# Row sends moved out of the ends of two outer stages, into the last inverse and the first 28 expert tiles

## The chip, the cores and the metric

One core of a Trainium2 chip runs the kernel. The metric is the device time of one execution in microseconds. The kernel before took 2111.44 us, the median of 3 runs (2107.42 to 2115.52).

## The reference

Two parts run one after the other. The first is a long convolution over 4 batches of 11456 tokens with 128 channels, done with transforms: `u = x * v`, its transform times the transform of a filter `h_filt` made by a small network from `pos_emb`, transformed back to `y`, cut to the sequence, and `x * y` handed on. The second is a mixture of 8 experts over the 45824 tokens: `logits = x @ w_gate + modality_bias[modality_id]`, the expert of a token is the `argmax`, `gate_w` its softmax weight, and `out = gate_w * (relu(x @ w1[e]) @ w2[e])` for the tokens of expert `e`.

## The kernel before

**The convolution.** A transform is split in two. An outer stage runs 16 steps q over the channels; a middle stage runs 23 groups g (`NG`) of frequencies. Outer stage b (0 to 4) does two things in one step: `product` and `transform` bring batch b in, and `inverse` (`turn`, `transform` of `inverse_stages`) takes batch b-1 out. Outer stage 0 has no inverse, outer stage 4 (the last inverse) has no product. Between outer stage b and the next stands middle stage b: `spectrum` (PE L646), `products` (DVE L663 and L670; POOL L665, L666, L676, L677), `inverse` (PE L701). With the inverse runs the routing of its tokens, one block `o` of 16 columns in two steps: `shift` on POOL (L808, L810) prepares the biases in `lg`, `biased` on DVE (L817) adds the logits to them, `choice` finds the expert, `send` computes where each token's row goes, and `store` writes rows to DRAM (`xr`).

**The rows.** The finished rows of a batch have to be put in the order of their expert, in `xs`. A batch has 90 pieces of 128 rows, numbered here batch.piece (0.0 to 3.89): 360 sends. `send_rows` (L283) is an indirect DMA that POOL issues; it takes a piece from `waiting`, reads it from one of three `back` tiles, each of 5 pieces, and writes it to `xs`. The load of a `back` tile (`rows_back`, L263) is issued on POOL too, behind the second piece of the tile before it. `paced` sends n pieces that also wait for a given DVE instruction. A batch comes into `waiting` (`fetch`) once its rows are stored and at most 5 pieces are left of the batch before. Sends stand at four kinds of places:

- in outer stages 2 and 3, `product` sends 2 or 3 a step and `inverse` 1 on each of two DVE instructions (L743, L746);
- in middle stages 2 and 3, `products` sends 7 in all, from group 13 on;
- in the last inverse, `inverse` sends 2 or 3 a step;
- in the expert part, a tile sends 4 until tile 12 and 3 afterwards, until all are gone.

**The experts.** Tiles of 512 rows of one expert run through 8 chunks c of the hidden layer. PE, ACT and DVE work on a tile; SP reads its rows (`x<-xs`, L1121 or L1125), writes its result `oT` to `ob` and reads it back as `y` (2 buffers). POOL multiplies `y` by the gate (L1290) and issues 4 indirect DMAs of results, `out<-ot` (L1292). The first 37 tiles (`NW0`) need batches 0 and 1 only, so the first `x<-xs` waits for sends 0.0 to 1.89; tiles to 59 need three batches. From tile 50 on, `rest` waits for all 360 sends, writes rows of padding behind each expert's rows (SP, L1052 and L1060) and makes the table for the tiles from 60 on. Those writes stand on SP's queue ahead of the rows of tile 53.

**What sets the order.** The order on PE, ACT, DVE and SP is that in which the program is written. POOL's is not: a scheduler places its instructions, and a send that the program writes in a middle stage can stand ahead of that stage's first products.

Of the kernel before, what the change touches and what calls it, by code (L numbers as in the profile page):

```python
# [67 lines left out]
NDYN = 8  # L68
NA, NXO = 12, 3
NPE = 9  # L70


def apart(a, axis):
# [116 lines left out]
def hyena_moe_kernel(ctx: ExitStack, tc: tile.TileContext, a: dict, out: bass.AP,  # L190
                     nb: int = B, nt: int = NF + NH):
    nc = tc.nc
    pe, act, dve, pool, sp = nc.tensor, nc.scalar, nc.vector, nc.gpsimd, nc.sync
# [14 lines left out]
    def bank(name):  # L208
        return banks[-1].tile([D, 512], F32, tag="ps", name=name)
# [7 lines left out]
    def sm(name):  # L217
        lo, hi = SMALL[name]
        return small[:, lo:hi]
# [22 lines left out]
    def ins_of(x):  # L242
        return getattr(x, "ins", x)
# [21 lines left out]
    def fetch(b):  # L265

        sp.dma_start(to_t[b % 2], xi[b].rearrange("(p c) -> p c", p=D))
        rows_back(b, 0)
        waiting.extend((b, c) for c in range(NR // D))
# [109 lines left out]
    with ExitStack() as cv:  # L379
# [5 lines left out]
        def pair(name):  # L385
            return pairs.tile([D, 2, 512], F32, tag="pp", name=name)
# [4 lines left out]
        def new_a(key):  # L391

            taken[key] = tiles.pop(0)
            return taken[key]

        def free(*keys):

            tiles.extend(taken.pop(key) for key in keys)
# [62 lines left out]
        def xo_of(b, o):  # L461

            return xo_t[(NO * b + o) % NXO]

        def paced(x, n=1):

            send_rows(n, wait=ins_of(x))

        def four(src, w=2):

            return src.rearrange("p (w n d) -> p w n d", w=w, n=4)

        def forward_stages(b):
            kept = {}

            def load(q):
                for name in ("u", "v"):
                    if b == 0 and name == "v":
                        of = xo_t[q // 2 % NXO].rearrange("p w s h r -> p (w s h r)")
                        t = of[:, 1024 * (q % 2):1024 * (q % 2) + 1024]  # L480
                    else:
                        t = new_a((name, q))
                    kept[q, name] = t
                    sp.dma_start(t[0:D:2], a[name][b, q, 0:D // 2])
                    sp.dma_start(t[1:D:4], a[name][b, q, D // 2:])

            def product(q):

                u = kept[q, "u"]
                s = dve.scalar_tensor_tensor(u, u, sm("held")[:, 0:1], kept.pop((q, "v")),  # L490
                                             op0=ALU.mult, op1=ALU.mult)
                paced(s, 2 + (q % 2 == 0))
                if b:
                    free(("v", q))

            def transform(q):

                u = kept.pop((q, "u")).rearrange("p (b d n) -> p b d n", b=2, n=N2)
                for h in range(2):
                    p = pair("s1")  # L500
                    v = p[:, :, 0:4 * N1].rearrange("p b (d k) -> p b d k", d=4)
                    for j in range(4):
                        for blk in range(2):
                            for c in range(2):
                                pe.matmul(v[64 * c:64 * c + 64, blk, j], u[:, blk, 4 * h + j],  # L505
                                          fwd[:, c], start=True, stop=True)
                    d0 = 8 * q + 4 * h
                    act.copy(A.rearrange("p k b d -> p b k d")[:, :, :, d0:d0 + 4],
                             v.rearrange("p b d k -> p b k d"))
                free(("u", q))  # L510

            return load, product, transform
# [204 lines left out]
        def inverse_stages(b):  # L717

            kept = {}
            w_of = lambda q, blk: w_t[blk + 2 * (q % 2 if b == nb - 1 else 0)]  # L720

            def load(q):
                t = kept[q] = new_a(("x", q))
                sp.dma_start(t, a["x"][b, q])

            def turn(q, blk):
                for c in range(2):
                    p = bank("wt")
                    for j in range(4):
                        pe.transpose(p[0:N1, D * j:D * j + D], A[:, :, blk, 8 * q + 2 * j + c], ident)  # L730
                    act.copy(w_of(q, blk)[:, c], p[0:N1])

            def transform(q):


                py = pair("py")
                for c in range(2):
                    for blk in range(2):
                        pe.matmul(py[64 * blk:64 * blk + 64, c], inv[:, c], w_of(q, blk)[:, c],
                                  start=True, stop=True)  # L740
                y = new_a(("y", q))
                act.copy(y[:, 512:1024], py[:, 1])
                paced(dve.tensor_add(y[:, 0:512], py[:, 0], y[:, 512:1024]),  # L743
                      1 + (b == nb - 1 and q % 2))
                dve.tensor_sub(y[:, 512:1024], py[:, 0], y[:, 512:1024])
                paced(dve.tensor_mul(xo_of(b, q // 2)[:, :, q % 2, :, 0:D], four(y),  # L746
                                     four(kept.pop(q))))
                free(("x", q), ("y", q))

            return load, turn, transform  # L750
# [329 lines left out]
    kept = {}  # L1080
# [10 lines left out]
    def experts(lo, hi):  # L1091
# [5 lines left out]
        def rows_in(i):  # L1097
# [10 lines left out]

            by_pe = k["by_pe"] = i < NPE or i == last or n < T
            x = mt.tile([D, 4, RW], F32, tag="x", name="x", bufs=4)  # L1110
# [193 lines left out]
        for at in range(len(work) + 6):  # L1304
            i, c = work[at] if at < len(work) else (last + 1, at - len(work))
            if c == 0:
                rows_in(i + 2)
            hidden(at)
            if at < 2:
                weights(lo, 2 + at)  # L1310
            if lo == 0 and 0 <= at - FL < len(finale):
                finale[at - FL](late)
            if lo == 0 and at >= FL + len(finale) + 2 and len(waiting) <= RC and not fetched:
                fetched.append(fetch(nb - 1))
            if lo == 0 and c % (2 if i < 12 else 3) == 0:
                send_rows(1)
            if lo == 0 and 1 <= i and c % 3 == 0:
                whole_weights(1)
            if 8 <= i < NW0:
                next(second, 0)  # L1320
            if NW1 - 10 <= i < NW1:
                next(others, 0)
            if c < 4:
                weights(i + 1, c)
            result(at - 3)
            whole = i <= last and tiles[i][2] == T
            if c == (3 if whole else 1):
                rows_turn(i + 1)
            if c == (4 if whole else 2):
                rows_split(i + 1)  # L1330
            if c == 2 and i - 2 in by_act:
                rows_out(i - 2)
            if c == (5 if whole else 3) and i - 1 not in by_act:
                rows_out(i - 1)
# [52 lines left out]
```

## Time and profile before

| | |
|---|---|
| median of 3 runs | 2111.44 us (2107.42 to 2115.52) |
| profiled execution | 2110.57 us, span 2108.7 us |
| mean granted TensorE clock | 0.986 |
| PE busy | 2022.3 us, 96% |
| DVE busy | 1675.1 us, 79% |
| POOL busy | 1369.1 us, 65% |
| ACT busy | 1192.9 us, 57% |
| 360 sends `xs<-back` on POOL (L283) | 389.4 us busy, 1082 ns each |
| 362 issues `out<-ot` on POOL (L1292) | 392.1 us busy, 1083 ns each |

The busy share of POOL is a mean over stages: in the expert part it has hardly a gap while rows are sent, at other times it waits. In rows of the trace the bracket at the end is the time that the engine sat idle before the instruction, and what released it. "issue" there is time in which it waited for nothing that the profile shows. Outer stage 2 ends at about 610 us, outer stage 3 at about 863 us; the last inverse runs from about 985 to 1075 us.

### The profile page before, as it was taken

How to read it: one execution, taken by the hardware profiler on the slowest of the kernel's cores; microseconds unless marked ns; L12 is line 12 of the kernel's file. 1: busy time of each engine (PE TensorE's matmuls, PEld its weight loads, DVE VectorE, ACT ScalarE, POOL GpSimd, SP SyncE). 2: the span in 40 equal slices, each digit the busy share in tenths (PEclk: the TensorE clock that was granted, in tenths of full speed). 3: DMA queues.
4: the chain of work that ended last, by engine and by line, in shares of the span. 5: the costliest groups of instructions: out<-in, count | busy, mean ns of one | idle time of the engine just before them, and what ended most of it. 6: DMA issues, size and time to landing. Idle time of an engine off the chain costs nothing. (4 is left out here: it accounts for less than half of the span.)

```text
span 2108.7 us, 49645 instructions
## 1 busy us (share of the span) xinstructions
PE 2022.3 (96%) x17794; PEld 1653.7 (78%) x17794; DVE 1675.1 (79%) x2663; ACT 1192.9 (57%) x2174; POOL 1369.1 (65%) x1496
## 2 busy tenths in 40 slices
PE   8999999999978999699999999999999999999997
PEld 8887877777757877488668888888888888888897
DVE  2538867996767967497887899988999999899885
ACT  3642476226631266223766666666666666666775
POOL 2219600796778876787667887888888665555554
PEclk9999999999989999899999999999999999999998
DMA  9846766678975788666689466666655554554310
GB/s 290 304 167 237 244 205 185 229 250 271 286 234 190 255 267 278 195 228 215 182 261 305 106 132 131 133 133 134 136 132 125 122 113 96 100 99 99 81 41 30
DMA packets 502932, 380.74 MB, mean 181 GB/s; under 512 B 374745, under 2 KB 408365, under 8 KB 502681
## 3 DMA queue, kind: packets, MB, share of 16 engines
q1 hardware_dynamic: 470265, 294.16, 51.0%
q0 software_dynamic: 32256, 83.33, 11.8%
q8 instruction: 142, 2.33, 0.4%
q14 instruction: 109, 0.89, 0.1%
q10 hardware_dynamic: 160, 0.03, 0.0%
HBM read 273.80 MB, written 103.96 MB: 179 GB/s over the span
## 5 line engine op out<-in xcount | busy, mean ns | idle before, releaser
L1240 DVE SCALAR_TENSOR_TENSOR hl<-ph,hh 128x512 fp32r<-128x512 f32 x724 | 484.7, 680 | 93.9 <-ACT hh L1239 85.0
L1239 ACT ACTIVATE hh<-ph 128x512 fp32r<-128x512 f32 x724 | 424.5, 598 | 200.9 <-PE ph L1236 193.1
L283 POOL DMA_INDIRECT xs<-back,to x360 | 389.4, 1082 | 175.8 <-issue 87.2
L1292 POOL DMA_INDIRECT out<-ot,idx x362 | 392.1, 1083 | 128.6 <-issue 82.0
L1234 PE MATMUL ph<-xh,wh 128*128 128x512 f32 (+1 forms) x792 | 298.5, 377 | 1.1 <-ACT xh L1220 1.1
L1236 PE MATMUL ph<-xl,wh 128*128 128x512 f32 (+1 forms) x792 | 296.1, 374 | 2.4 <-DVE xl L1221 2.4
L1235 PE MATMUL ph<-xh,wl 128*128 128x512 f32 (+1 forms) x792 | 294.4, 372 | 1.0 <-DVE wl L1189 1.0
L1257 PE MATMUL po<-hh,wh 128*128 128x512 f32 (+1 forms) x792 | 294.4, 372 | 0.0
L1259 PE MATMUL po<-hl,wh 128*128 128x512 f32 (+1 forms) x792 | 293.9, 371 | 0.0
L1258 PE MATMUL po<-hh,wl 128*128 128x512 f32 (+1 forms) x792 | 293.7, 371 | 0.0
L701 PE MATMUL pw<-rings,a 64*128 64x128 f32 x3952 | 242.1, 278 | 38.0 <-POOL a L676 33.9
L701 PEld LDWEIGHTS pw<-rings,a 64*128 64x128 f32 x3952 | 230.6, 191 | 57.3 <-POOL a L676 36.4
L707 ACT COPY A<-pw 128x512 f32<-128x512 f32 x180 | 95.7, 584 | 317.7 <-PE pw L701 317.7
L670 DVE TENSOR_TENSOR a<-pz,rings 128x1024 f32<-128x1024 f32 (+1 forms) x184 | 211.5, 1191 | 1.0 <-POOL a L677 1.0
L646 PE MATMUL pz<-A,rings 128*64 128x256 f32 x1440 | 170.0, 384 | 13.4 <-issue 8.9
L1236 PEld LDWEIGHTS ph<-xl,wh 128*128 128x128 f32 x792 | 149.4, 189 | 31.0 <-DVE xl L1221 3.5
L505 PE MATMUL s<-fwd,a 128*64 128x90 f32 x4096 | 170.1, 242 | 1.2 <-issue 1.1
L1235 PEld LDWEIGHTS ph<-xh,wl 128*128 128x128 f32 x792 | 149.6, 189 | 26.3 <-DVE wl L1189 1.3
L1234 PEld LDWEIGHTS ph<-xh,wh 128*128 128x128 f32 x792 | 149.4, 189 | 26.3 <-ACT xh L1220 1.3
L1257 PEld LDWEIGHTS po<-hh,wh 128*128 128x128 f32 x792 | 149.1, 188 | 26.0 <-issue 0.7
L1259 PEld LDWEIGHTS po<-hl,wh 128*128 128x128 f32 x792 | 149.1, 188 | 25.8
L1258 PEld LDWEIGHTS po<-hh,wl 128*128 128x128 f32 x792 | 149.1, 188 | 25.3
(192 smaller groups left out, 3537.7 us busy)
## 6 DMA issues: line engine op xcount, KB each, us to landing
rings<-hs SPq DMA_DIRECT2D x88, 512.0 KB
a<-in_x SPq DMA_DIRECT2D x64, 512.0 KB
xr<-xo SPq DMA_DIRECT2D x64, 365.6 KB
back<-xr POOLq DMA_DIRECT2D x72, 325.0 KB
rings<-in_c_b SPq DMA_DIRECT2D x88, 256.0 KB
rings<-in_c_c SPq DMA_DIRECT2D x88, 256.0 KB
x<-xs SPq DMA_DIRECT2D x292, 64.0 KB
ob<-oT SPq DMA_DIRECT2D x292, 64.0 KB
```

Source lines behind the costliest of these rows:

```text
L283: s = pool.indirect_dma_start(out=xs, out_offset=bass.IndirectOffsetOnAxis(ap=ix, axis=0), in_=src, in_offset=None, bounds_check=E * R - 1 ...
L670: dve.tensor_mul(part[i], z[:, :, i].unsqueeze(1).broadcast_to([D, 2, n, 2, D]), h[:, 0].unsqueeze(3).broadcast_to([D, 2, n, 2, D]))
L701: pe.matmul(pw[par][:, to:to + D], t[at], k["c"][at, q, c], start=i == 0, stop=i == len(terms) - 1)
L1234: pe.matmul(p, k[0, "h"][:, f:f + D], k["xh"], start=True, stop=False)
L1235: pe.matmul(p, k[0, "l"][:, f:f + D], k["xh"], start=False, stop=False)
L1236: pe.matmul(p, k[0, "h"][:, f:f + D], k["xl"], start=False, stop=True)
L1239: act.activation(hh, ph, AF.Relu)
L1240: dve.scalar_tensor_tensor(hl, ph, 0.0, hh.bitcast(F32), op0=ALU.max, op1=ALU.subtract)
L1257: pe.matmul(po, k[1, "h"][:, f], hh[:, t], start=g == 0, stop=False)
L1258: pe.matmul(po, k[1, "l"][:, f], hh[:, t], start=False, stop=False)
L1259: pe.matmul(po, k[1, "h"][:, f], hl[:, t], start=False, stop=g == NCH - 1)
L1292: s = pool.indirect_dma_start(out=out, out_offset=bass.IndirectOffsetOnAxis(ap=k["idx"][:, j:j + 1], axis=0), in_=ot[:, j, :], in_offset=N ...
```

## The change

A number `QS = 13` is new. In outer stages 2 and 3 the steps q = 13, 14 and 15 send nothing, neither beside the product nor beside the inverse: 13 pieces fewer in each stage. In the last inverse each step sends 3, two on L743 and one on L746 (48 in all, 40 before). In the expert part tiles send 4 until tile 28, not 12. Line numbers after line 71 are one higher than before.

```
--- before.py
+++ after.py
@@ -68,6 +68,7 @@
 NDYN = 8
 NA, NXO = 12, 3
 NPE = 9
+QS = 13
 
 
 def apart(a, axis):
@@ -489,7 +490,7 @@
                 u = kept[q, "u"]
                 s = dve.scalar_tensor_tensor(u, u, sm("held")[:, 0:1], kept.pop((q, "v")),
                                              op0=ALU.mult, op1=ALU.mult)
-                paced(s, 2 + (q % 2 == 0))
+                paced(s, 2 + (q % 2 == 0) if q < QS else 0)
                 if b:
                     free(("v", q))
 
@@ -740,11 +741,11 @@
                                   start=True, stop=True)
                 y = new_a(("y", q))
                 act.copy(y[:, 512:1024], py[:, 1])
-                paced(dve.tensor_add(y[:, 0:512], py[:, 0], y[:, 512:1024]),
-                      1 + (b == nb - 1 and q % 2))
+                n = 1 if b == nb - 1 or q < QS else 0
+                paced(dve.tensor_add(y[:, 0:512], py[:, 0], y[:, 512:1024]), n + (b == nb - 1))
                 dve.tensor_sub(y[:, 512:1024], py[:, 0], y[:, 512:1024])
                 paced(dve.tensor_mul(xo_of(b, q // 2)[:, :, q % 2, :, 0:D], four(y),
-                                     four(kept.pop(q))))
+                                     four(kept.pop(q))), n)
                 free(("x", q), ("y", q))
 
             return load, turn, transform
@@ -1312,7 +1313,7 @@
                 finale[at - FL](late)
             if lo == 0 and at >= FL + len(finale) + 2 and len(waiting) <= RC and not fetched:
                 fetched.append(fetch(nb - 1))
-            if lo == 0 and c % (2 if i < 12 else 3) == 0:
+            if lo == 0 and c % (2 if i < 28 else 3) == 0:
                 send_rows(1)
             if lo == 0 and 1 <= i and c % 3 == 0:
                 whole_weights(1)
```

With that, 28 pieces of batch 0 wait at the end of outer stage 2 (15 before), 52 of batches 0 and 1 at the end of outer stage 3 (26 before), and the expert part begins with 183 sends done (201 before). The last send stands in tile 49 (48 before). The order on PE, DVE and ACT is the same; SP's differs only in where it loads the row numbers of a batch. POOL's order differs.

On POOL, at the end of outer stage 2, from the biases of routing block 5 (`lg_7032`) to those of block 6 (`lg_7270`), stood before:

```order
L808 TENSOR_TENSOR lg_7032<-wf_140,bias_143 109x128
L810 TENSOR_TENSOR lg_7032<-lg_7032,flagged_142 109x128
L808 TENSOR_TENSOR flagged_142<-wf_140,bias_143 109x128
L283 DMA xs_66<-back0_94,to0_92 373248x130 x2
L263 DMA back1_95<-xr0_58 128x650
L283 DMA xs_66<-back0_94,to0_92 373248x130 x3
L283 DMA xs_66<-back1_95,to0_92 373248x130 x2
L263 DMA back2_96<-xr0_58 128x650
L283 DMA xs_66<-back1_95,to0_92 373248x130 x2
L808 TENSOR_TENSOR lg_7270<-wf_140,bias_143 109x128
L810 TENSOR_TENSOR lg_7270<-lg_7270,flagged_142 109x128
```

Now, from block 5 (`lg_7020`) to block 6 (`lg_7229`), with the tile that a send reads named `back0` to `back2`:

```order
L809 TENSOR_TENSOR lg_7020<-wf_140,bias_143 109x128
L284 DMA xs_66<-back0_94,to0_92 373248x130
L811 TENSOR_TENSOR lg_7020<-lg_7020,flagged_142 109x128
L284 DMA xs_66<-back0_94,to0_92 373248x130
L809 TENSOR_TENSOR flagged_142<-wf_140,bias_143 109x128
L284 DMA xs_66<-back0_94,to0_92 373248x130 x3
L264 DMA back1_95<-xr0_58 128x650
L284 DMA xs_66<-back1_95,to0_92 373248x130 x2
L264 DMA back2_96<-xr0_58 128x650
L284 DMA xs_66<-back1_95,to0_92 373248x130 x2
L809 TENSOR_TENSOR lg_7229<-wf_140,bias_143 109x128
L811 TENSOR_TENSOR lg_7229<-lg_7229,flagged_142 109x128
```

Nine sends and two loads stood between the two blocks, and nine sends and two loads stand there now, but other ones: three sends written in middle stage 2 (the first of them between L809 and L811 of block 5) are ahead of step 12's, and the load of `back1` has the first read of `back1` right behind it.

On POOL, behind block 6's biases, up to the first products of middle stage 2 (L665), stood before:

```order
L283 DMA xs_66<-back2_96,to0_92 373248x130 x2
L263 DMA back0_94<-xr0_58 128x650
L283 DMA xs_66<-back2_96,to0_92 373248x130 x3
L283 DMA xs_66<-back0_94,to0_92 373248x130 x2
L263 DMA back1_95<-xr0_58 128x650
L808 TENSOR_TENSOR lg_7358<-wf_140,bias_143 109x128
L283 DMA xs_66<-back0_94,to0_92 373248x130
L810 TENSOR_TENSOR lg_7358<-lg_7358,flagged_142 109x128
L283 DMA xs_66<-back0_94,to0_92 373248x130 x2
L283 DMA xs_66<-back1_95,to0_92 373248x130
L665 TENSOR_TENSOR a2_125<-a2_125 128x256
L666 TENSOR_TENSOR a2_125<-a2_125 128x256
```

Now:

```order
L809 TENSOR_TENSOR flagged_142<-wf_140,bias_143 109x128
L809 TENSOR_TENSOR lg_7317<-wf_140,bias_143 109x128
L811 TENSOR_TENSOR lg_7317<-lg_7317,flagged_142 109x128
L666 TENSOR_TENSOR a2_125<-a2_125 128x256
L667 TENSOR_TENSOR a2_125<-a2_125 128x256
```

One send ahead of the rows of before, the eleven in them and one behind them (it stood ahead of L676) make thirteen, and all are gone from there; what is left is the biases. At the end of outer stage 3 the order changes in the same way, with three loads (two of them read right behind) ahead of block 6.

On POOL, in the last inverse, around the last piece of batch 1 (the last `to1` row), stood before:

```order
L263 DMA back2_96<-xr1_59 128x650
L283 DMA xs_66<-back1_95,to1_93 373248x130 x3
L283 DMA xs_66<-back2_96,to1_93 373248x130
L808 TENSOR_TENSOR lg_12036<-wf_140,bias_143 109x128
L810 TENSOR_TENSOR lg_12036<-lg_12036,flagged_142 109x128
L808 TENSOR_TENSOR flagged_142<-wf_140,bias_143 109x128
L283 DMA xs_66<-back2_96,to1_93 373248x130 x4
L283 DMA xs_66<-back0_94,to0_92 373248x130
L808 TENSOR_TENSOR lg_12183<-wf_140,bias_143 109x128
L810 TENSOR_TENSOR lg_12183<-lg_12183,flagged_142 109x128
L808 TENSOR_TENSOR flagged_142<-wf_140,bias_143 109x128
L283 DMA xs_66<-back0_94,to0_92 373248x130
```

Now, `lg_12527` being the last block's biases:

```order
L284 DMA xs_66<-back1_95,to1_93 373248x130
L264 DMA back2_96<-xr1_59 128x650
L284 DMA xs_66<-back1_95,to1_93 373248x130 x3
L284 DMA xs_66<-back2_96,to1_93 373248x130 x2
L809 TENSOR_TENSOR lg_12527<-wf_140,bias_143 109x128
L811 TENSOR_TENSOR lg_12527<-lg_12527,flagged_142 109x128
L809 TENSOR_TENSOR flagged_142<-wf_140,bias_143 109x128
L811 TENSOR_TENSOR bs_late_110<-bs_late_110,flagged_142 109x128
L284 DMA xs_66<-back2_96,to1_93 373248x130 x3
L284 DMA xs_66<-back0_94,to0_92 373248x130 x2
```

Piece 1.89 stood ahead of the biases of `lg_12183`, three blocks before the last one; it now stands behind the last block's.

On POOL, at the end of the sends, in the expert part, stood before:

```order
L283 DMA xs<-back_95,to_93 373248x130
L283 DMA xs<-back_96,to_93 373248x130 x2
L1280 CAST idx<-ends 128x4
L1290 TENSOR_TENSOR ot<-y,ends 128x512
L1292 DMA out<-ot,idx 45824x128 x4
L283 DMA xs<-back_96,to_93 373248x130 x3
L1280 CAST idx<-ends 128x4
L1290 TENSOR_TENSOR ot<-y,ends 128x512
L1292 DMA out<-ot,idx 45824x128 x4
L1280 CAST idx<-ends 128x4
L1290 TENSOR_TENSOR ot<-y,ends 128x512
```

Now:

```order
L284 DMA xs<-back_96,to_93 373248x130 x3
L1281 CAST idx<-ends 128x4
L1291 TENSOR_TENSOR ot<-y,ends 128x512
L1293 DMA out<-ot,idx 45824x128 x4
L284 DMA xs<-back_96,to_93 373248x130 x2
L1281 CAST idx<-ends 128x4
L1291 TENSOR_TENSOR ot<-y,ends 128x512
L1293 DMA out<-ot,idx 45824x128 x4
L1281 CAST idx<-ends 128x4
L1291 TENSOR_TENSOR ot<-y,ends 128x512
```

The last send stands one tile later, so one more tile's cast, product and four `out` stand ahead of it.

## Rows read from the trace of the kernel before

**Rows 1.** The page: busy time, share of the span and instructions by engine
```profile
PE 2022.3 (96%) x17794; PEld 1653.7 (78%) x17794; DVE 1675.1 (79%) x2663; ACT 1192.9 (57%) x2174; POOL 1369.1 (65%) x1496
```

**Rows 2.** Windows: us, busy time (count) by engine, granted clock, DMA share, GB/s
```profile
620.00:630.00 10.00, 0.83 (x4) 0.51 (x3) 1.98 (x4) 0.00 (x0) 5.52 (x8) 0.50 0.95 354
```

**Rows 3.** Timeline of POOL, outer to middle stage 2: start, duration, idle before
```profile
592.43 0.42 POOL L808 TENSOR_TENSOR lg<-wf,bias 109x128 f32<-109x128 f32 x1
...
609.87 0.45 POOL L810 TENSOR_TENSOR lg<-lg,flagged 109x128 f32<-109x128 f32 x1
...
615.64 0.59 POOL L263 DMA_DIRECT2D back<-xr  x1 [1.09 <-issue]
...
623.65 0.97 POOL L283 DMA_INDIRECT xs<-back,to  x1 [3.57 <-DMA back<-xr]
```

**Rows 4.** Timeline of DVE at the same place
```profile
610.36 0.29 DVE L817 TENSOR_TENSOR lg<-lt,lg 109x128 f32<-109x128 f32 x1 [3.88 <-POOL lg L810]
...
614.80 2.35 DVE L670 TENSOR_TENSOR a<-pz,rings 128x1024 f32<-128x1024 f32 x2
...
645.07 1.29 DVE L663 TENSOR_TENSOR a<-pz,rings 128x512 f32<-128x512 f32 x2 [12.69 <-PE pz L646]
```

**Rows 5.** Timeline of PE at the same place
```profile
617.25 2.46 PE L646 MATMUL pz<-A,rings 128*64 128x256 f32 x16 [2.11 <-issue]
619.64 1.19 PE L801 MATMUL lt<-ident,lT_late 128*109 128x128 f32 x4
637.41 0.80 PE L701 MATMUL pw<-rings,a 64*128 64x128 f32 x4 [16.58 <-POOL a L676]
```

**Rows 6.** Timeline of POOL, outer to middle stage 3
```profile
829.95 0.60 POOL L263 DMA_DIRECT2D back<-xr  x1
...
862.69 0.45 POOL L810 TENSOR_TENSOR lg<-lg,flagged 109x128 f32<-109x128 f32 x1
...
869.85 0.59 POOL L263 DMA_DIRECT2D back<-xr  x1
...
877.70 0.97 POOL L283 DMA_INDIRECT xs<-back,to  x1 [4.69 <-DMA back<-xr]
```

**Rows 7.** Timeline of PE, beginning of middle stage 3
```profile
889.05 0.80 PE L701 MATMUL pw<-rings,a 64*128 64x128 f32 x4 [16.47 <-POOL a L676]
```

**Rows 8.** Timeline of POOL in the last inverse
```profile
1032.10 1.29 POOL L283 DMA_INDIRECT xs<-back,to  x1 [0.30 <-issue]
...
1061.27 0.59 POOL L263 DMA_DIRECT2D back<-xr  x1
...
1068.63 0.97 POOL L283 DMA_INDIRECT xs<-back,to  x1 [2.37 <-DVE xo L852]
```

**Rows 9.** Timeline of DVE, step 14 of the last inverse
```profile
1070.11 1.23 DVE L746 TENSOR_TENSOR xo<-a,a 128x1024 f32<-128x1024 f32 x1
```

**Rows 10.** Timelines of SP and PE, beginning of the expert part
```profile
1067.09 0.33 SPq L1121 DMA_DIRECT2D x<-xs  x1
...
1072.65 0.66 PE L1210 MATMUL px<-ident,x 128*128 128x128 f32 x4
```

**Rows 11.** POOL by line, 1119 to 1638 us: count, busy, mean, idle before
```profile
L1292 POOL DMA_INDIRECT out<-ot,idx x181 | 195.5, 1080 | 54.4 <-issue 35.3 <-POOL ot L1290 10.6 <-DMA x<-xs 3.7
L283 POOL DMA_INDIRECT xs<-back,to x151 | 156.1, 1034 | 45.7 <-issue 45.1 <-DVE hl L1240 0.6
L1290 POOL TENSOR_TENSOR ot<-y,ends 128x512 f32<-128x512 f32 x38 | 40.3, 1059 | 0.0
```

**Rows 12.** Timeline of POOL, end of the sends
```profile
1636.91 0.97 POOL L283 DMA_INDIRECT xs<-back,to  x1 [0.30 <-issue]
```

**Rows 13.** Timelines of SP and DVE, from the last send to tile 53
```profile
1640.17 0.37 SPq L1052 DMA_DIRECT2D xs<-pad  x1
...
1659.35 1.97 SPq L1125 DMA_DIRECT2D x<-xs  x4
...
1663.47 0.71 DVE L1212 STREAM_TRANSPOSE xT<-x 128x512 f32<-128x512 f32 x1 [1.11 <-DMA x<-xs]
```

More of the change, by code (lines that the diff above doesn't have):

```diff
@@ L70 @@
 NPE = 9
+QS = 13
 def apart(a, axis):
@@ L491, in product @@
                                              op0=ALU.mult, op1=ALU.mult)
-                paced(s, 2 + (q % 2 == 0))
+                paced(s, 2 + (q % 2 == 0) if q < QS else 0)
                 if b:
@@ L742, in transform @@
                 act.copy(y[:, 512:1024], py[:, 1])
-                paced(dve.tensor_add(y[:, 0:512], py[:, 0], y[:, 512:1024]),
-                      1 + (b == nb - 1 and q % 2))
+                n = 1 if b == nb - 1 or q < QS else 0
+                paced(dve.tensor_add(y[:, 0:512], py[:, 0], y[:, 512:1024]), n + (b == nb - 1))
                 dve.tensor_sub(y[:, 512:1024], py[:, 0], y[:, 512:1024])
                 paced(dve.tensor_mul(xo_of(b, q // 2)[:, :, q % 2, :, 0:D], four(y),
-                                     four(kept.pop(q))))
+                                     four(kept.pop(q))), n)
                 free(("x", q), ("y", q))
@@ L1314, in experts @@
                 fetched.append(fetch(nb - 1))
-            if lo == 0 and c % (2 if i < 12 else 3) == 0:
+            if lo == 0 and c % (2 if i < 28 else 3) == 0:
                 send_rows(1)
```

## The prediction

> **What bounds the kernel now.** The page comes first: PE is busy for 96% of the span, POOL for 65% [rows 1]. By that share POOL has room. The share is a mean, though, so the next thing to read is which engine PE waits for where it does wait, and what POOL does in each stage.
>
> PE's timeline shows one long stop at the start of middle stage 2: the first inverse matmul waited 16.58 us for POOL's L676 [rows 5], and at middle stage 3 the same wait is 16.47 us [rows 7]. In the window from 620 to 630 us PE was busy for 0.83 of 10 us, at a granted clock of 0.50, the lower of its two levels [rows 2]. What POOL did meanwhile is in its timeline: it was putting out sends, and stood still for a load of `back` that was issued at 615.64 and let the send go on only at 623.65, 8.0 us after its issue [rows 3]; at 869.85 and 877.70 the same took 7.85 us [rows 6], in the last inverse 7.4 [rows 8].
>
> In the expert part, from 1119 to 1638 us, POOL's groups show 181 `out`, 151 sends and 38 products, with idle time before them that is nearly all "issue", 0.30 us an instruction [rows 11]. So POOL waits for nobody there; it sets its own pace, while PE never stops. That stretch ends with the last send at 1636.91 [rows 12]. Behind it stand the pads at 1640.17, and behind the pads, on SP, the rows of tile 53 at 1659.35. DVE's transpose of them at 1663.47 had waited 1.11 us [rows 13]. That is small, but it says that the chain last send, pads, tile 53 is already just late. What makes the last send later makes the end later.
>
> So POOL's sends bound two kinds of places, the starts of middle stages 2 and 3 and the way to tile 53. The change takes sends from the first and gives them to the second.
>
> **Start of middle stage 2.** The thirteen sends behind block 6's biases go, and PE's stop with them, were nothing late behind. But the order puts three sends of the middle stage ahead of those of step 12, so that the load of `back1` is read by the very next instruction. The count on POOL from block 5's biases at 592.43 [rows 3]: biases with their gaps 1.9 (three operations like the 0.42 and 0.45 of that view), five sends at 1.034 + 0.30 = 1.33 each [rows 11] 6.7, so the load goes at 601.0. With 8.0 us to the send behind it [rows 3]: 609.0. Two sends, a load and two sends, 6.2, then L809 and its gap: block 6's L811 starts at about 615.7, against 609.87 before. DVE's L817, which waited 3.88 us for it at 610.36 [rows 4], waits some 5.8 more, and behind it on DVE stand block 6's routing and the first products. These end at 614.80 + 2.35 + 5.8 = 622.9 [rows 4]. PE's spectrum of group 2 began 0.1 us behind that end, at 617.25, and with the transposes behind it was done at 620.83 [rows 5]; now 626.6. There inverse0 can go: at 626.6 instead of 637.41, **G2 = 11 us**. Were the landing hidden, inverse0 could go at 620.8: 16.6, the upper bound. The lower bound is 9, with sends that take 1.5 us instead of 1.03.
>
> The Trainium skill's page "DMA: Bandwidth & Descriptors", section "Anatomy of one DMA — SWDGE (gpsimd) path", fits a transfer issued by GpSimd with 2.0 us plus its bytes at 436 GB/s. For the 325 KB of a load that is an estimate of 2.8 us, and by it the landing would nearly hide and G2 would be 16. The trace's 8.0, 7.85 and 7.4 us do not agree, with the DMA engines 95% busy in the window of the first; I go by the trace.
>
> **Start of middle stage 3.** The same, with two loads that are read right behind. From the load at 829.95 [rows 6]: the landing 8.0, five sends 6.7, biases 1.9, a send 1.3, a load with its landing 8.0, two sends and a load 3.6, four sends 5.3, L809 0.5: block 6's L811 starts at 865.3, or at 867.3 with sends of 1.5 us, against 862.69 [rows 6]. It is late by 2.6 to 4.6, and the stop of 16.47 [rows 7] shrinks by the rest, 11.9 to 13.9. I take **G3 = 11**, the same as G2, since its second landing falls into the same transfers; the bounds are 9 and 16.5.
>
> **Last inverse and first tile.** A step sends 3. Five pieces cost POOL 5 x 1.33 + 0.6 for the load + 1.6 for their share of the biases = 8.9 us, while 1.67 steps of 5.6 us (16 steps in about 90 us) give 9.4. That fits alone, but a load has only three sends and at times biases to hide in, 4 to 6 us of its 7.4 [rows 8], so that most tiles of `back` lose 1 to 2.4 us; over the nine or ten of them POOL falls some 10 us behind. Piece 1.89, which the first `x<-xs` needs, went at 1032.10 [rows 8]; now it waits for step 14, whose L746 ends at 1071.34 [rows 9], and for POOL's lag: 1073 to 1084 on the old clock. The first rows were loaded at 1067.09 and turned at 1072.65 [rows 10]. With 1 us for the send and 2 to 4 for its landing and the load's, they are turned at 1080 to 1092: 7 to 19 later. I take the middle, **D = 13**. On PE, which waits with the first transposes, all tiles stand behind this.
>
> So the expert part begins 11 + 11 - 13 = 9 us earlier.
>
> **The expert part.** POOL is without a pause from tile 1's first `out` to the last send, so its added work is added time. The sends: 18 x 1.33 = 24.0 [rows 11]. Four more loads at 0.6 [rows 3]: 2.4. One more tile's work ahead of the last send: four `out` at 1.08 + 0.30, a product of 1.06 [rows 11] and a cast of about 0.3, 6.9. Sum 33.3 us. More sends a tile from 12 to 28 do not help: they only change the order in which POOL does the same work, and make its results lag more. As no slack is left at tile 53 [rows 13], the last send comes 33.3 - 9 = 24.3 us later, and the pads, tile 53 and the end with it. PE's stop moves to tiles 50 to 53 and is about 25 us long. What it costs to come out of the lower clock there I leave out of the sum, up to 2.5 us, and keep for the range.
>
> Profiled execution: 2110.57 + 24.3 = 2134.9. The median is 0.9 above it; rounded, the forecast is **2135 us**.
>
> **Rivals.** (a) The landings hide (loads land in 3 us as the transfers have less beside them). For it speaks that PE's and SP's loads of the middle stage stand elsewhere; against it, three landings of 7.4 to 8.0 in three stages. Then G2 + G3 - D = 16.6 + 16.5 - 7 = 26, the last send comes 7 us later, 2119 us: no change that can be told. (b) The way to tile 53 does not bind. It is a mechanism of its own on SP: if the 1.11 us there came from SP's place in PE's time rather than from the last send, `y` and `ot` buffers would take up POOL's lag, PE would go on, and only the gain in the outer stages would count. It decides if the last send may come some 24 us later without a stop of PE. Against it, SP's queue holds tile 53 behind the pads, whatever PE does. Price: the 9 us, up to 26 with (a): 2085 to 2102, about 2100. (c) The last inverse cannot keep up at all, D over 25 as the loads collide with the rows stored and read: over 2149.
>
> **Chances.** Forecast 0.68, spread over 2122 to 2149; (a) 0.19; (b) 0.09; (c) 0.04. The range reaches from 2109, in which (a) lies, to 2149, where D is at 19, G2 and G3 are at 9 and the clock's 2.5 is paid: 33.3 + 1 + 2.5 = 37. The forecast's own range is 2122 to 2149. A change under 0.5%, 10.5 us, cannot be told from none here. Slower 0.70: the forecast with a part of its lower edge left to "same", and (c). Same 0.21: (a) and that edge. Faster 0.09: (b).
>
> **What would show it.** In the changed profile: a wait of POOL of over 5 us for `back` ahead of block 6 in outer stages 2 and 3; PE's waits for POOL at middle stages 2 and 3 down from 16.6 and 16.5 to 7 or less; the first `x<-xs` at least 7 us later, counted from the last inverse's start; POOL without a pause to the last send, 33 us longer from tile 1's first `out`; a stop of PE for tile 53's rows of some 25 us, at the lower clock. The forecast is wrong if PE does not stop there, or if G2 + G3 - D is over 22.

## The result, and the profile after

The changed kernel takes 2131.78 us (median of 5 runs, 2124.85 to 2133.26) against 2112.1 us before (5 runs): ratio 1.0086, 95% interval 1.0062 to 1.0109. It is 20 us slower. The forecast was 2135, range 2109 to 2149. The profiled execution has a span of 2129.9 us, 21.2 more than before; the mean granted clock is 0.985.

The start of one and the same instruction in both profiles shows where the 21.2 us arose. The columns are routing adds on DVE (L817 before, L818 now) behind middle stages 1, 2 and 3, and results on DVE (L1265, L1266) of tiles 9, 45 and 60; the entry is the start in the kernel named less the start in the kernel before, in us.

| kernel | after middle 1 (512) | after middle 2 (764) | after middle 3 (1011) | tile 9 (1203) | tile 45 (1595) | tile 60 (1758) |
|---|---|---|---|---|---|---|
| changed | +1.1 | -12.8 | -26.5 | -9.5 | -7.8 | +21.1 |
| pads from tile 54 | -0.1 | -11.7 | -25.7 | -13.6 | -10.8 | +2.8 |
| before, pads from tile 54 | -0.5 | -1.0 | -0.4 | -0.7 | -0.7 | +2.5 |
| loads two tiles ahead | +2.8 | -14.9 | -28.6 | -8.2 | -5.7 | +23.7 |
| both | +4.4 | -12.9 | -26.0 | -5.5 | -4.7 | +7.5 |
| only stage 2 empty | -2.6 | -15.6 | -14.6 | -10.5 | -2.6 | +1.0 |
| before, 4 a tile to tile 28 | -1.9 | -0.6 | -1.4 | -1.7 | +5.5 | +4.3 |
| table first | -3.0 | -17.9 | -31.7 | -14.8 | -14.8 | -10.1 |
| table first, 4 to tile 20 | 0.0 | -12.3 | -26.6 | -9.6 | -9.7 | -7.3 |
| before, table first | +1.5 | +2.5 | +4.0 | +3.7 | +3.7 | +4.6 |
| stage 2, table first, 4 to tile 12 | +0.6 | -13.3 | -17.0 | -17.1 | -17.1 | -16.5 |
| QS = 14, table first, 4 to tile 20 | -0.5 | -11.8 | -21.8 | -18.8 | -18.9 | -17.6 |

The first column says how far two profiles differ ahead of any change, a few us; differences along a row are what counts. In the row of the changed kernel, with the forecast's G2, G3 and D: G2 is 1.1 + 12.8 = 13.9, G3 is 26.5 - 12.8 = 13.7, D is 26.5 - 9.5 = 17.0, and from tile 9 to tile 60 it loses 30.6.

Some rows are the same program for a long way, and show how far one profile can be trusted. Up to tile 20 "changed", "pads from tile 54", "table first" and "table first, 4 to tile 20" do not differ: their G2 is 13.9, 11.6, 14.9 and 12.3, their G3 13.7 to 14.3, their D 17.0, 12.1, 16.9 and 17.0. The two rows with stage 2 alone are the same up to tile 12: G2 13.0 and 13.9, G3 -1.0 and 3.7, D 4.1 and -0.1. A term taken from one row is good to some 3 to 5 us.

**Start of middle stage 2.** POOL's timeline of the changed kernel (start, duration, idle before), to be read against [rows 3]:

```profile
602.75 0.61 POOL L264 DMA_DIRECT2D back<-xr  x1
609.48 1.16 POOL L284 DMA_INDIRECT xs<-back,to  x1 [6.13 <-DMA back<-xr]
...
615.61 0.45 POOL L811 TENSOR_TENSOR lg<-lg,flagged 109x128 f32<-109x128 f32 x1
...
622.94 1.28 POOL L677 TENSOR_TENSOR a<-a,a 128x512 f32<-128x512 f32 x1 [0.80 <-DVE a L671]
```

The load of 602.75 is followed by a send that stood 6.13 us for it, and block 6's biases come at 615.61; the forecast had 615.7. DVE and PE behind them:

```profile
616.10 0.29 DVE L818 TENSOR_TENSOR lg<-lt,lg 109x128 f32<-109x128 f32 x1 [6.33 <-POOL lg L811]
...
620.51 2.35 DVE L671 TENSOR_TENSOR a<-pz,rings 128x1024 f32<-128x1024 f32 x2
...
631.92 1.29 DVE L664 TENSOR_TENSOR a<-pz,rings 128x512 f32<-128x512 f32 x2 [0.49 <-PE pz L647]
```

```profile
622.96 2.84 PE L647 MATMUL pz<-A,rings 128*64 128x256 f32 x16 [3.63 <-issue]
...
626.86 3.13 PE L702 MATMUL pw<-rings,a 64*128 64x128 f32 x48
```

DVE's routing add waited 6.33 us, more than the 3.88 of [rows 4]; the first products follow at once, and inverse0 goes at 626.86 without a wait, where it had waited 16.58 us until 637.41 [rows 5].

**Start of middle stage 3.** POOL, and PE's inverse0:

```profile
824.07 0.61 POOL L264 DMA_DIRECT2D back<-xr  x1
...
829.89 1.47 POOL L284 DMA_INDIRECT xs<-back,to  x1 [3.56 <-DMA back<-xr]
...
839.91 0.60 POOL L264 DMA_DIRECT2D back<-xr  x1
843.43 1.78 POOL L284 DMA_INDIRECT xs<-back,to  x1 [2.92 <-DMA back<-xr]
...
854.52 0.45 POOL L811 TENSOR_TENSOR lg<-lg,flagged 109x128 f32<-109x128 f32 x1
```

```profile
864.36 2.95 PE L702 MATMUL pw<-rings,a 64*128 64x128 f32 x48
```

Of the two loads on which a send soon waits, one costs 3.56 us (a send stands between) and the other 2.92; from issue to that send they take 5.8 and 3.5 us, less than the 8.0 in the forecast's count. The biases at 854.52 are still late: the kernel before had them at 862.69 [rows 6], and 12.8 us of that are gone at middle stage 2, which leaves 849.9. Inverse0 at 864.36 is 24.7 ahead of 889.05 [rows 7], 11.9 without the 12.8.

**Last inverse and first tile.** POOL (the last row is piece 1.89), a routing add on DVE, SP's first rows, PE's first transposes, and PE's wait for them in total:

```profile
1032.36 0.98 POOL L284 DMA_INDIRECT xs<-back,to  x1 [0.30 <-issue]
...
1039.54 0.58 POOL L264 DMA_DIRECT2D back<-xr  x1 [4.44 <-DVE used L364]
...
1056.31 0.98 POOL L284 DMA_INDIRECT xs<-back,to  x1 [0.30 <-issue]
```

```profile
1041.11 0.29 DVE L818 TENSOR_TENSOR lg<-lt,lg 109x128 f32<-109x128 f32 x1 [2.12 <-POOL lg L811]
```

```profile
1058.85 0.33 SPq L1122 DMA_DIRECT2D x<-xs  x1
```

```profile
1062.01 1.09 PE L1211 MATMUL px<-ident,x 128*128 128x128 f32 x4 [14.38 <-DMA x<-xs]
```

```profile
PE px L1211 <- DMA x<-xs: 14.4, 1, 14.4
```

Piece 1.89 left at 1056.31, on this kernel's clock some 26 us ahead of the kernel before's, so at 1083 on the old one; before it was 1032.10 [rows 8]. PE stood 14.4 us for the rows, and DVE's routing add 2.12 us for POOL's biases: 16.5 of the 17.0 of D. PE's long waits for POOL at the middle stages, 16.58 and 16.47 us [rows 5, 7], are gone from its list.

**The expert part.** POOL from tile 1's first `out`, 1105.17, to the last send (columns as in [rows 11]):

```profile
L1293 POOL DMA_INDIRECT out<-ot,idx x188 | 202.9, 1079 | 62.7 <-issue 40.8 <-POOL ot L1291 10.8 <-DMA x<-xs 6.6
L284 POOL DMA_INDIRECT xs<-back,to x169 | 173.1, 1024 | 51.2 <-issue 50.3 <-DVE wl L1190 0.3 <-DVE hl L1241 0.3
L1291 POOL TENSOR_TENSOR ot<-y,ends 128x512 f32<-128x512 f32 x39 | 41.5, 1065 | 0.0
```

Its sends take 1.02 us and 0.30 idle, 1.03 and 0.30 before. The stretch is 1659.26 - 1105.17 = 554.1 us long, against 1637.88 - 1114.63 = 523.25 before: 30.8 more, with 18 sends, four `out`, four loads and a product more (counted from the same place the kernel before has 184 `out`; [rows 11] begin 4.4 us later). How it ends, on POOL, SP, DVE and PE:

```profile
1658.28 0.98 POOL L284 DMA_INDIRECT xs<-back,to  x1 [0.31 <-issue]
```

```profile
1643.66 0.61 SPq L1052 DMA_DIRECT2D pad<-in_c_pad  x1
1660.60 0.37 SPq L1053 DMA_DIRECT2D xs<-pad  x1
...
1664.01 2.10 SPq L1270 DMA_DIRECT2D ob<-oT  x4
...
1678.64 1.97 SPq L1126 DMA_DIRECT2D x<-xs  x4
```

```profile
1667.71 0.72 DVE L1266 STREAM_TRANSPOSE oT<-po 128x512 f32<-128x512 f32 x1 [13.16 <-DMA ob<-oT]
...
1682.62 0.71 DVE L1213 STREAM_TRANSPOSE xT<-x 128x512 f32<-128x512 f32 x1 [12.96 <-DMA x<-xs]
```

```profile
1669.06 0.79 PE L1260 MATMUL po<-hl,wh 128*128 128x512 f32 x1 [11.42 <-DVE off L332]
...
1683.96 0.79 PE L1260 MATMUL po<-hl,wh 128*128 128x512 f32 x1 [11.97 <-DVE off L334]
```

SP issued the load of its pad at 1643.66 and could write the first pad only at 1660.60, behind the last send. On DVE tile 51's result waited 13.16 us for the stores of tile 50's (`ob<-oT`), which stand on SP behind the first pads, and tile 53's rows came 12.96 us late. PE stopped twice for it, 11.42 and 11.97 us. In the windows of those 20 us it did next to nothing, at a granted clock of 0.58 and 0.50 (busy time, then clock, DMA share, GB/s):

```profile
1660.00:1670.00 10.00, 0.94 (x2) 0.83 (x3) 1.95 (x4) 0.00 (x0) 4.63 (x6) 0.58 0.47 125
1670.00:1680.00 10.00, 1.99 (x5) 0.99 (x3) 0.00 (x0) 0.00 (x0) 5.01 (x5) 0.50 0.28 90
```

### The profile page after: what moved, and what is told of

Its sections match the earlier page's. It is cut to its first block, busy times and chain, and to the rows that moved or that the text cites. A ratio compares the mean times of both kernels' runs of the same rounds, so it can differ in the third digit from the quotient of the medians.

```text
span 2129.9 us, 49636 instructions
## 1 busy us (share of the span) xinstructions
PE 2030.2 (95%) x17794; PEld 1654.7 (78%) x17794; DVE 1675.1 (79%) x2663; ACT 1191.8 (56%) x2174; POOL 1365.7 (64%) x1496
## 3 DMA queue, kind: packets, MB, share of 16 engines
q0 software_dynamic: 32256, 83.33, 11.8%
## 5 line engine op out<-in xcount | busy, mean ns | idle before, releaser
L702 PE MATMUL pw<-rings,a 64*128 64x128 f32 x3952 | 237.5, 275 | 4.6 <-ACT A L708 1.4
```

Of the source, the lines that this page charges most:

```text
L702: pe.matmul(pw[par][:, to:to + D], t[at], k["c"][at, q, c], start=i == 0, stop=i == len(terms) - 1)
```

## The experiments

Edits are against the changed kernel unless the kernel before is named.

**Pads from tile 54.**

```
-            if NW1 - 10 <= i < NW1:
+            if NW1 - 6 <= i < NW1:
                 next(others, 0)
```

> The changed kernel, but the pads and the last table are begun at tile 54 and not at tile 50. Theory: the loss is the way last send, pads, tile 53 on SP's queue. The last send still lands at about 1658 us, but SP asks for it some 44 us later, so both stops of PE (11.4 and 12.0 us) go and what is left is the 9.5 us that the expert part begins earlier: 2102 us, ratio 0.995 to before. Rival: POOL's added work is itself the bound, as its results lag by 41 us and the two y buffers stop PE: then PE stops for POOL's products and the time stays at 2125 or more.

> The kernel before, with the pads begun at tile 54. Theory: its last send came in time, only 1 to 2 us were lost there: 2110 to 2112 us, ratio 0.999 to 1.000. Rival: the pads cost time by being late wherever they stand, then the kernel before gains as much as the changed one does.

Measured: 2115.32 us for the changed kernel, ratio to before 1.0017 (1.0004 to 1.003), and 2114.28, ratio 1.0022 (1.0008 to 1.0035), for the kernel before. So by the medians 16.5 of the 20 us of loss hang on where the pads stand, and in the kernel before nothing was lost there: it became 2 us slower, and missed its 2110 to 2112. The 2102 was not reached either. Two rows of SP in the first kernel show a part of the rest, its waits from 1620 to 1760 us (total, times, longest) and its timeline at the pads:

```profile
SPq L1272 <- POOL ot L1291: 10.9, 4, 4.4
```

```profile
1678.82 0.61 SPq L1052 DMA_DIRECT2D pad<-in_c_pad  x1
1681.55 0.37 SPq L1053 DMA_DIRECT2D xs<-pad  x1
...
1699.53 1.97 SPq L1126 DMA_DIRECT2D x<-xs  x4
```

POOL's results were 40 us behind, so SP waited for a `y` buffer, with the next tiles' rows behind it on its queue; and from 1678.82 to 1699.53 SP was taken by the load of the pad, eight of the nine pads and the stores of one result. The first theory was right on the stop, and left out that SP had no slack for the pads.

**Loads two tiles ahead.**

```
         rows_back(b, 0)
+        rows_back(b, 1)
...
-            if c % RC == 1 and c // RC + 1 < NB:
-                ld = rows_back(b, c // RC + 1)
+            if c % RC == 2 and c // RC + 2 < NB:
+                ld = rows_back(b, c // RC + 2)
```

> The changed kernel, with each load of back issued two tiles ahead (behind the third send of the tile before the one before it), so that five to seven sends lie between a load and its first read. Theory: the landing of 7 to 8 us right ahead of a send sets G2, G3 and most of D. G2 and G3 go from 13.9 and 13.7 to about 16.5, D from 17 to 7 to 10, tile 53 comes 12 to 15 us earlier: 2117 to 2120 us, ratio 1.003. The stops at tiles 51 and 53 shrink to about 10 us in all. Rival: the first send behind a load is late for another reason (the DVE instruction that it waits for, the order of POOL): then the time stays within 4 us of 2132.

> Both edits, loads two tiles ahead and pads from tile 54. Theory: the gains at the middle stages and at the first tile all reach the end: 9.5 + 12 to 15 us under the kernel before, 2088 to 2091 us, ratio 0.989. Rival: with the stop gone, POOL's lag limits PE and little is left of either: 2102 or more.

Measured: 2135.11 us, ratio 1.0107 (1.0083 to 1.013), and with pads from tile 54 2119.19, ratio 1.0034 (1.0017 to 1.005). The theory fell, and both times are where the rivals have them. G2 did grow, from 13.9 to 17.7, but G3 stayed at 13.7 and D went from 17.0 to 20.4. POOL at the end of outer stage 2, and in the last inverse:

```profile
611.16 0.58 POOL L264 DMA_DIRECT2D back<-xr  x1 [2.53 <-DVE a L746]
...
612.24 1.33 POOL L812 TENSOR_TENSOR lg<-lg,flagged 109x128 f32<-109x128 f32 x1
```

```profile
1040.21 0.58 POOL L264 DMA_DIRECT2D back<-xr  x1 [4.31 <-DMA xs<-back,to]
...
1057.52 0.98 POOL L285 DMA_INDIRECT xs<-back,to  x1 [0.30 <-issue]
```

Two loads wait there and hold POOL up, 2.53 and 4.31 us. The second is the first load of batch 2, which overwrites a `back` tile and waits until the sends that read this tile have landed: the last of them was issued at 1033.63 and landed, by its semaphore, at 1039.76. What the 2.53 us are stays open: the sends that read that load's tile had landed by 603.0. Piece 1.89 left at 1057.52, no earlier than in the changed kernel. What sets it there is not the landing of loads: from the first send of the last inverse to piece 1.89 the changed kernel's POOL shows

```profile
L284 POOL DMA_INDIRECT xs<-back,to x45 | 49.3, 1096 | 26.5 <-DVE a L745 10.4 <-issue 8.6 <-DVE a L746 1.7
L264 POOL DMA_DIRECT2D back<-xr x9 | 5.4, 603 | 4.4 <-DVE used L364 4.4
```

45 sends of 1.10 us with 0.30 at each, nine loads and 10.6 us for biases come to some 79 of 88 us. The wait of 9.4 us for DVE's L745 lies ahead of the first send, which is paced, and so ahead of the 88; the kernel before has the same wait. In POOL's waits of that stretch the landing has 0.6 us:

```profile
POOL back L264 <- DVE used L364: 4.4, 1, 4.4
...
POOL xs L284 <- DMA back<-xr: 0.6, 2, 0.3
```

The 4.4 us ahead of the load at 1039.54 are put down to a DVE instruction, but it is the same wait of the same load, the first of batch 2: POOL's queue was held until 1038.69 by the semaphore of the send of 1032.36, the last that reads the same `back` tile, which landed at 1038.66, 6.3 us after its issue. With three waits of 0.8 to 2.2 us it makes up the other 9 of the 88. In the kernel with the pads from tile 54, the same program to here, this load did not stop POOL (a send ahead of it waited 2.3 us), and D is 12.1.

**Only stage 2 empty.** In stage 3 the product and the inverse send again at q >= 13:

```
-                paced(s, 2 + (q % 2 == 0) if q < QS else 0)
+                paced(s, 2 + (q % 2 == 0) if q < QS or b != 2 else 0)
...
-                n = 1 if b == nb - 1 or q < QS else 0
+                n = 1 if b != 1 or q < QS else 0
```

**4 a tile to tile 28 alone**, in the kernel before:

```
-            if lo == 0 and c % (2 if i < 12 else 3) == 0:
+            if lo == 0 and c % (2 if i < 28 else 3) == 0:
```

> The changed kernel, but outer stage 3 sends again in its last three steps, as before; only outer stage 2 sends nothing there. Theory (the sum, term by term): G2 of 13.9 us stays, G3 is 0. The expert part begins with 196 sends done; piece 1.89 goes 13 pieces, 4.3 steps, earlier than in the changed kernel, so the first rows are not late and D falls from 17 to 0 to 2. The last send stands in tile 45, so POOL has 5 sends more and 3 tiles' results less ahead of it than in the kernel before, and nothing stops PE for tile 53. 2112 - 12 to 14: 2098 to 2100 us, ratio 0.994. Rival: sends taken out of an outer stage come back elsewhere whatever their number, so the time is 2110 or more.

> The kernel before, with only the third edit: 4 sends a tile until tile 28. Theory: it changes only in which tile POOL does its sends; the last one stands in tile 43, the way to tile 53 gets slack that the kernel before does not use, PE is the bound in between: 2110 to 2113 us. Rival: results that lag by over 35 us hold up SP, which waits for the y buffers with the next tiles' rows behind it: 2116 or more.

Measured: 2109.46 us, ratio 0.9997 (0.9987 to 1.0007), and 2118.13, ratio 1.0046 (1.0031 to 1.006). Both misses have in the main one cause. In the table's row the first kernel has G2 of 13.0, D of 4.1 (0 to 2 expected), and tile 9 at -10.5; by tile 45 it is at -2.6. The second loses 7 between tiles 9 and 45. No long stop of PE shows, only windows that are not quite full (in the kernel before PE is busy for 100.00 in both), and SP's waits in the same 200 us:

```profile
1380.00:1480.00 100.00, 98.30 (x430) 79.84 (x429) 87.59 (x135) 64.65 (x116) 79.64 (x84) 1.00 0.60 129
1480.00:1580.00 100.00, 99.22 (x431) 79.74 (x430) 90.85 (x133) 63.91 (x116) 81.35 (x87) 1.00 0.59 130
```

```profile
SPq L1271 <- POOL ot L1290: 63.1, 17, 6.3
```

In both kernels the results lag on POOL (from the transpose of `oT` to the product L1290) by up to 44 us, 16 to 22 in the kernel before at the same tiles. With two `y` buffers SP then waits for POOL. That alone is not the loss: with the table first SP waits 60.7 us in the same 200 and PE loses nothing. What tells them apart is DVE's wait for the next tiles' rows, from tile 9 to tile 45 in the kernel before with 4 a tile to tile 28, and in the changed kernel with the table first:

```profile
DVE xT L1212 <- DMA x<-xs: 14.6, 14, 2.3
```

```profile
DVE xT L1213 <- DMA x<-xs: 0.4, 1, 0.4
```

Between these tiles the kernels line up by it (us; the lag is the longest):

| kernel | lag | SP waits for POOL's results | DVE waits for rows | lost |
|---|---|---|---|---|
| before | 22.1 | 0.2 | 0 | 0 |
| QS = 14, table first, 4 to tile 20 | 34.8 | 59.3 | 0 | 0 |
| table first | 41.2 | 67.3 | 0.4 | 0 |
| changed | 41.3 | 72.0 | 4.5 | 1.7 |
| pads from tile 54 | 41.5 | 74.0 | 8.8 | 2.8 |
| before, 4 a tile to tile 28 | 42.9 | 89.9 | 14.6 | 7.2 |
| only stage 2 empty | 44.2 | 92.0 | 17.1 | 7.8 |

Up to some 67 us of SP's waits rows come late for 0.4 us at most and nothing is lost; from there on the loss grows with DVE's wait for rows. So the third edit is not free: alone it costs 6 to 8 us.

**The table first, the pads spread out.** The lines of `rest` that write the pads move behind those that make the table, and the pads come one every three chunks:

```
                       scatters)
-            yield
...
+            yield from range(3)
```

> The changed kernel; from tile 50 on the table of the last tiles is made first and the pads come behind it, one every three chunks instead of one a chunk, from about tile 53 on. Theory: in the run with the pads at tile 54, some 7 us were lost as SP waited for y buffers, and 10 as nine pads in a row held up the rows of tile 57. Spread out, the pads cost 0 to 3: 2105 to 2109 us. Rival: the lag of POOL's results is the whole of that loss, and the time stays at 2113 to 2117.

> As the run with the table first, but with 4 sends a tile only until tile 20. The sends end in tile 52 instead of 49, and POOL's results lag by some 8 sends (10 us) less at tile 28: about 30 us instead of 40. Theory: SP then does not wait for y buffers, and the 9.5 us that the expert part begins earlier reach the end: 2101 to 2104 us. Rival: the pads cost what they cost (10 us in a row): 2109 or more; or, with the last send three tiles later, PE stops for it again: 2115 or more.

> The kernel before, with the table first and the pads behind it, one every three chunks. Theory: its last send was in time, so it gains no more than the 1 to 2 us that it lost at tile 53: 2110 to 2112 us, ratio 0.999 to 1.000; then the 9 to 10 us of the run with the table first are those of the changed sends. Rival: the pads in a row cost every kernel 5 us or more, then this one comes to 2105 or less and the sends are worth less than 9.5.

Measured: 2100.87 us, ratio 0.9956 (0.9943 to 0.9969); with 4 a tile to tile 20 only, 2101.59, ratio 0.9961 (0.9942 to 0.998); the kernel before with the table first 2112.59, ratio 1.0001 (0.999 to 1.0012). The first is faster than its 2105 to 2109, the other two are about where they were expected. So the changed kernel's loss is all in its way from the last send to tile 53: with that way out of the path the same sends gain 9 us (ratio 0.9956), and the kernel before gains nothing from the edit. The edit both starts the pads later and spreads them out; which of the two does it no run shows. Between tiles 45 and 60 4.7 us are still lost in the first of them, whose results lag by up to 41 us, 2.4 in the second, with up to 31, and 0.9 in the third, which has the same pads and a lag of up to 23.

**Two combinations.** Stage 2 alone with the table first and 4 a tile to tile 12; and `QS = 14` with the table first and 4 a tile to tile 20.

> Only outer stage 2 sends nothing at its end, 3 a step in the last inverse, 4 a tile until tile 12 as before, table first. Theory: G2 of 13, D of 4 as in the run with stage 2 alone, POOL's results lag by 25 to 30 us and not by 44, so that SP does not wait for y and the 10 us reach the end: 2099 to 2102 us. Rival: if not the lag but the number of sends in the expert part slows it, 2107 or more.

> QS is 14 instead of 13 (9 pieces fewer in a stage instead of 13), 4 a tile until tile 20, table first. Theory: in POOL's order no load is read right behind any more; block 6's biases come at about 616 as with 13, so G2 and G3 stay at 12 to 14 each, while piece 1.89 is 8 pieces earlier, so D falls from 17 to 3 to 7. The expert part begins 18 to 22 us earlier than in the kernel before: 2090 to 2094 us, ratio 0.991. Rival: D does not come from piece 1.89 but from POOL's casts and outs at the first tiles: then D stays at 15 or more and the time at 2101 or more.

Measured: 2097.12 us, ratio 0.9941 (0.9922 to 0.996), and 2093.62, ratio 0.9912 (0.9896 to 0.9929), the fastest here, 18 us under the kernel before. The first is faster than its 2099 to 2102. Stage 2's gain reaches the end once neither lag nor pads are in its way: from tile 9 to tile 60 0.6 us are lost, 11.5 in the run with stage 2 alone. That is most of the 12 us between the two medians; the other 6.6 by which tile 9 is ahead (-17.1 for -10.5) arose where the two programs are the same. In the second, piece 1.89 is 8 pieces earlier. G2 and G3, 11.3 and 10.0, are under the 12 to 14 expected, but D is 3.0 and not 17, and PE's wait for the first rows is

```profile
PE px L1211 <- DMA x<-xs: 1.4, 1, 1.4
```

against 14.4 us. D fell by 14.0 us and this wait by 13.0, so most of D is the wait for piece 1.89.

## Why the prediction was right

**The bound (right).** POOL's sends hold up both kinds of places. Its added work up to the last send was 30.8 us (forecast 33.3) and became added time about one for one (30.6 us from tile 9 to tile 60), though POOL is busy for only 64% of the span.

**G2 and G3 (right way, too small).** 13.9 and 13.7 for 11 and 11, inside the bounds of 9 to 16.5; other profiles of the same program have 11.6 to 14.9 and 13.7 to 14.3. At middle stage 2 block 6's biases came at 615.61, which is 614.5 without the 1.1 of the table, for 615.7, and inverse0 at 626.86 for 626.6: a landing of 6.7 us for 8.0 made up for most of a load issued at 602.75 for 601.0. At stage 3 two errors cancel as well. The load from which the forecast counts came at 824.07 and not at 817.2 (829.95 less the 12.8 gained by then), and the way from it to the biases took 30.5 us for 35.4, with landings of 5.8 and 3.5 for 8.0 twice. The biases were 4.6 us late, the edge of the 2.6 to 4.6 forecast. The sign "over 5 us for `back`" came at outer stage 2 (6.13) and not at 3 (3.56 and 2.92).

Up to inverse0 the gains are 11.7 (with the 1.1 of the table) and 11.9, near the forecast. Two us more arise right behind it, the step that the forecast left out. The changed kernel does all 48 matmuls of inverse0 in 3.13 us (626.86 above); the kernel before, coming out of its stop at the lower clock [rows 2], took 0.80 for the first 4 [rows 5] and for the others

```profile
638.62 4.52 PE L701 MATMUL pw<-rings,a 64*128 64x128 f32 x44 [0.42 <-POOL a L677]
```

at a granted clock of 0.50 until 642 us, so that the next products on DVE are 13.2 us earlier (631.92 for 645.07 [rows 4]). The forecast had counted the lower clock as a cost of the new stop, and not as a gain where a stop goes. Its price for that, "up to 2.5 us", is worked out from no row that it names; these rows show 2.6 (5.7 us for 3.13), 0.42 of them a wait for POOL.

The loads of `back` took 6.7, 5.8 and 3.5 us here. The Trainium skill's page "DMA: Bandwidth & Descriptors", section "Anatomy of one DMA — SWDGE (gpsimd) path", gives by its fit an estimate of 2.8 us for one of them; the 3.5 is near it, the 6.7 is not.

Three readings of the forecast do not hold as they stand. The 7.4 us of the last inverse are more than the landing: the row's wait was ended by DVE (`<-DVE xo L852` [rows 8]), and by its semaphore the load had landed 6.6 us after its issue. The bounds for sends "that take 1.5 us instead of 1.03", 9 for G2 and 867.3, come out with 1.5 in place of 1.33, the 0.30 between sends included; with 1.5 + 0.30 for the nine and twelve sends counted there they would be 6.6 and 870.9. And 2134.9 + 0.9 is 2135.8, not 2135.

**D (size near, mechanism wrong).** 17.0 for 13, within 7 to 19. The step "most tiles of `back` lose 1 to 2.4 us" failed: POOL lost 0.6 us to landings there. "That fits alone" failed too: the forecast gave a step 5.6 us, but in the kernel before the 16 steps begin 5.2 us apart, so 1.67 of them are 8.6 us and not 9.4, less than the 8.9 that five pieces cost. In the changed kernel DVE's pace gives POOL 77.6 us from the first send to piece 1.89 (969.28 to 1046.92, the ends of the two instructions that they wait for), and POOL has 79 us of work. The pace leaves no room, so each wait adds to the lag, and the longest is the 4.4 us ahead of batch 2's first load. POOL was 9.4 us behind at piece 1.89: that this is about the 10 forecast is luck. Hence (a) also fell: with landings hidden, D was no smaller.

**The expert part (right sum, one step wrong).** The stop came, 11.42 + 11.97 = 23.4 us for the 25 forecast, in two pieces: the first is for tile 51's result, which waits for stores that stand on SP behind the first pads; the forecast did not name it. The clock cost about 2 us: tile 53's transpose is 19.15 later, the end 21.2, and the granted clock was 0.50 from 1684 to 1686 us and 0.65 from there to 1690. About 2 us of slack that the forecast put at zero were there: the last send is 21.4 later, the pads 20.4, the transpose 19.15. "More sends a tile from 12 to 28 do not help: they only change the order" was too mild: alone they cost 6 to 8 us, as SP waits for `y` buffers and rows come late. In the changed kernel that cost 1.7 us by tile 45, and nothing in the same program with the table first.

**Sum.** -13.9 - 13.7 + 17.0 + 1.1 (ahead of the change) + 30.6 = 21.1, where the forecast had 24.3. G gained 5.6 more, D lost 4.0 more, the expert part lost 2.7 less, and 1.1 is no part of the change: the errors partly cancel, and that the forecast was closer than its terms is luck. Its gain of 9 us for the start of the expert part is steadier than they are: in the four profiles of the same program tile 9 gains 9.6 to 13.5 over the first column. Rival (b) is refuted by the two kernels with the table first: tile 53 did bind.

## What to carry to other kernels

Before work is moved from one stage to another on the same engine, look whether that engine is the one that paces both; a mean share of 64% can hide two stages in which it has no gap. Ask of a gain at the front what must be reached behind it: here a store that all later loads queue behind turned 18 sends into a 23 us stop, and moving and spreading these stores made the same change a gain. A lag that buffers absorb is free up to a point: up to tile 45 35 us cost nothing here, 41 us 0 to 3, and 43 to 44 us 7 to 8, without one stop long enough to be seen in PE's list of waits. Before the difference of two profiles is put down to an edit, look how far two profiles of the same program differ.

## What the runs showed of the hardware that was not expected

The time from a load's issue on POOL's queue to the send that reads it was 6.7 us at 602.75, 5.8 at 824.07 and 3.5 at 839.91 in one profile, for the same 325 KB. By their semaphores the 72 loads of that profile landed 3.2 to 16.8 us after the issue, 4.2 in the median. Up to 8 us the longer ones go with busier DMA engines (between issue and landing the 16 engines were busy for 0.50 of the time in the median of the thirty under 4 us, for 0.94 in that of the nine of 6 to 8). The six of 12 to 17 us do not (0.55 to 0.90), and no run shows why.

A load that is to overwrite a `back` tile held POOL's queue until the sends that read the tile had landed: batch 2's first load for 4.4 us in the changed kernel, where the last of these sends landed 6.3 us after its issue, and for 4.3 us with the loads two tiles ahead, where it took 6.1.
